# Loading 320 tokens of the first batch ahead, the first pair through hardware queues, norm steps moved forward, and the last store in halves: attention and SwiGLU feed-forward in one kernel

## The chip, the cores and the metric

The kernel runs on one core of one Trainium2 chip. The metric is device time in microseconds (us) of one execution. Every version was run several times, alternating with the kernel before on the same chip. The granted clock is the share of full speed that the chip let TensorE run at, as the trace records it. Each run has a state, fast or slow, judged by its time and granted clock. All times below are of fast runs. One run of the kernel before, first listed beside the first four experiments, took 452.8 us at a granted clock of 0.849. It was in the slow state and is left out.

A trace counts from the start of its span, which leaves out about 1.8 us of the timed execution (span 405.8 us in a run of 407.61 us). Times within a trace are compared with times within a trace, and run times with run times.

## The reference, cut to what matters

Eight batches of blockwise causal attention (8 heads, 576 tokens, head size 64, blocks of 64) feed an RMS norm and a SwiGLU feed-forward layer (512 to 1536 to 512).

```python
scores = scale * np.matmul(q, k.transpose(0, 1, 3, 2))      # (8, 8, 576, 576)
mask = block_i >= block_j                                   # blocks of 64
attn = softmax(where(mask, scores, -1e9))
x = (attn @ v).transpose(0, 2, 1, 3).reshape(4608, 512)
xn = x / sqrt(mean(x * x) + 1e-6) * rms_g
g = xn @ w_gate
out = (g * sigmoid(g) * (xn @ w_val)) @ w_out
```

## The kernel before

TensorE (PE) does everything large. Attention is done per pair of heads: transpose q and k, multiply scores, and let ScalarE (ACT) take the exponential into `PT`; the product with v follows. A norm chain then runs over the tokens: sums, squares, a turn on VectorE (DVE), a root by Newton steps, a spread into `st`, and a scaling that multiplies by a broadcast of `st` and writes `XT`. A `group()` is one feed-forward step of 16 matmuls, or one down projection. The hand-written order puts groups between the attention steps so that PE has work while ACT and DVE finish theirs. `later(n, ...)` puts a step n groups further on. The results of matmuls go to tiles in PSUM (`fps`, `sps`). Batch 0 has nothing before it, so its order holds zero matmuls, `fill(n)`, instead of groups.

```python
    WARM = 11
    ...
    def fill(n):
        f = ps_f.tile([P, 512], FP32, name="fps")
        for _ in range(n):
            nc.tensor.matmul(f, zero[:, 0:P], zero, start=True, stop=True)

    fill(WARM)
    load_pair(0, 0)                  # q and k of heads 0, 1: GpSimd DMAs that cast to bf16
    make_identity(nc, ident)
    for t in range(1, HP):
        load_pair(0, t)
    ...
    transpose_pair(0, 0, on_act="k")
    ...
    fill(2)
    scores(0, 0, "a")
    scores(0, 0, "b")
    transpose_pair(0, 1, on_act="k")
    scores(0, 0, "c")
    fill(1)
    ...                              # pairs 1 to 3, first values, norm of the first 256 tokens
    group()
    scores(1, 0, 2)
    transpose_pair(1, 1, on_act="qk")
    for u in range(HP):
        norm_scale("b", 0, 256, 320, u)     # "the second scaling": tokens 256 to 575
    mark(S)
    scores(1, 1, 0)
    group()
```

The last down projection ends with one copy of 128 x 512 and two stores, both issued by SyncE (SP).

## Time and profile before

| | before |
|---|---|
| runs beside the changed kernel | 408.19 us median (407.38 to 408.34, 4 runs) |
| span of the trace | 405.8 us |
| PE busy | 388.2 us (96%) |
| granted clock of the profiled run | 0.999 |

The lines that the prediction rests on stand in it, below. Two more lines mattered in the end. The first is the page's row of the granted TensorE clock, in tenths of full speed, for 40 equal slices. The second comes from ACT's timeline; its columns are start, length, engine, line, what was done, and in brackets how long the engine idled before and what released it.

```profile
PEclk9999999999999999999999999999999999999999
```

```profile
1.19 1.28 ACT L204 ACT_TABLE_LOAD   x1 [1.19 <-PEq L721]
```

The clock stays at full rate throughout. ACT's function table is loaded in the first 2.5 us, when nobody needs ACT. The trace puts it down to line 204, the copy after the first transposes, but it ran four us before that copy.

### The profile page before, as it was taken

What the parts mean: (1) busy time and instruction counts of PE and PEld (TensorE: products, weight loads), DVE (VectorE), ACT (ScalarE), POOL (GpSimd) and SP (SyncE); (2) the same over time, 40 slices, a digit from 0 to 9 for tenths busy, and PEclk for the clock granted to TensorE, in tenths of its full rate; (3) what the DMA queues carried; (4) which work ended last, traced back from release to release, by engine and by line L of the source; (5) the groups of instructions that cost most, each with busy time, mean ns of one, the idle gap of its engine ahead of it and who ended that gap; (6) DMA issues with size and microseconds to landing.
All of it is one profiled execution on the core that took longest, in us unless ns stands there. A gap on an engine that the chain in (4) does not pass through costs nothing.

```text
span 405.8 us, 7824 instructions
## 1 busy us (share of the span) xinstructions
PE 388.2 (96%) x3090; PEld 183.1 (45%) x3090; DVE 252.1 (62%) x619; ACT 197.9 (49%) x284; POOL 128.7 (32%) x181
## 2 busy tenths in 40 slices
PE   7889999998999999999999999999999999999995
PEld 3567665433444444344444444444434434444442
DVE  4788585677767654477627765667457768554430
ACT  4826771475457653465446654565455213332321
POOL 8828675645047063660068004200110010100000
PEclk9999999999999999999999999999999999999999
DMA  8999999999929498998089905500120010010112
GB/s 110 172 204 185 193 145 140 184 151 160 108 58 129 60 91 132 133 144 104 2 119 139 135 12 86 71 0 2 40 67 2 0 37 17 20 33 27 52 53 78
DMA packets 139764, 36.43 MB, mean 90 GB/s; under 512 B 129232, under 2 KB 136912, under 8 KB 139728
## 3 DMA queue, kind: packets, MB, share of 16 engines
q0 software_dynamic: 108448, 26.75, 66.9%
q1 hardware_dynamic: 30752, 9.18, 16.1%
q8 instruction: 24, 0.39, 0.4%
q14 instruction: 12, 0.10, 0.1%
q10 hardware_dynamic: 528, 0.00, 0.1%
HBM read 38.80 MB, written 9.44 MB: 119 GB/s over the span
## 4 chain that ended last, share of the span: by engine, by line
PE 81%; DVE 10%; ACT 3%; DMA 2%; POOL 1%; issue 1%; DVEq 0%; ACTq 0%; POOLq 0%
PE fps L457 41%; PE fps L473 22%; PE sps L241 6%; PE sps L290 4%; PE fps L330 3%; DVE HT L465 3%; DVE gs L463 3%; DVE XT L426 2%; ACT th L461 2%; DMA VB<-in_v_dram 2%; PE fps L290 2%; PE fps L433 1%; PE fps L381 1%; POOL nt L109 1%; ACT PT L250 1%
## 5 line engine op out<-in xcount | busy, mean ns | idle before, releaser
L457 PE MATMUL fps<-XT,WG 128*128 128x512 bf16 (+1 forms) x480 | 113.3, 359 | 2.9 <-DVE XT L426 2.5
L463 DVE SCALAR_TENSOR_TENSOR gs<-th,fps 128x512 bf16<-128x512 f32 x108 | 74.1, 686 | 61.7 <-ACT th L461 61.4
L250 ACT ACTIVATE PT<-sps 128x1024 bf16<-128x1024 f32 (+1 forms) x96 | 93.4, 988 | 38.9 <-PE sps L241 38.4
L457 PE MATMUL fps<-XT,WV 128*128 128x512 bf16 (+1 forms) x480 | 111.0, 358 | 0.0
L461 ACT ACTIVATE th<-fps 128x512 f32<-128x512 f32 x108 | 64.6, 598 | 73.5 <-PE fps L457 71.3
L473 PE MATMUL fps<-WO,HT 128*128 128x512 bf16 x432 | 97.6, 380 | 0.3 <-DVE HT L465 0.3
L465 DVE TENSOR_TENSOR HT<-gs,fps 128x512 bf16<-128x512 bf16 x108 | 74.3, 688 | 11.6 <-DVE gs L463 0.5
L457 PEld LDWEIGHTS <-WV 128*128 128x128 bf16 x480 | 46.9, 98 | 49.0 <-issue 3.2
L457 PEld LDWEIGHTS <-WG 128*128 128x128 bf16 x480 | 42.4, 98 | 50.0 <-issue 14.1
L473 PEld LDWEIGHTS <-HT 128*128 128x128 bf16 x432 | 41.3, 98 | 51.9 <-issue 3.2
L476 ACT ACTIVATE osb<-fps 128x512 f32<-128x512 f32 x36 | 21.5, 597 | 81.2 <-PE fps L473 78.3
L484 POOL DMA_DIRECT2D out_dram<-osb x22 | 12.7, 575 | 149.2 <-ACT osb L476 147.0
L123 POOL DMA_DIRECT2D VB<-in_v_dram x48 | 39.6, 848 | 17.3 <-PE sps L290 14.2
L426 DVE SCALAR_TENSOR_TENSOR XT<-OT,gscale,fps 128x64 bf16<-128x64 bf16 (+5 forms) x72 | 30.2, 477 | 21.2 <-PE fps L433 21.2
L241 PE MATMUL sps<-QT,KT 64*128 64x192 bf16 (+5 forms) x280 | 32.1, 308 | 1.9 <-ACT KT L204 0.9
L116 POOL DMA_DIRECT2D nt<-in_q_dram x30 | 26.2, 875 | 7.0 <-DMA VB<-in_v_dram 4.6
L116 POOL DMA_DIRECT2D nt<-in_k_dram x30 | 26.3, 876 | 5.8 <-DMA nt<-in_q_dram 1.6
L290 PEld LDWEIGHTS <-VB 128*64 128x64 bf16 x344 | 14.3, 109 | 14.6 <-issue 4.7
L223 DVE MEMSET PT<- 64x64 uint32 x95 | 9.1, 112 | 18.6 <-ACT PT L250 15.3
L316 DVE TENSOR_TENSOR SQ<-OT 128x512 bf16<-128x512 bf16 (+1 forms) x44 | 16.0, 374 | 6.4 <-ACT OT L314 5.5
L487 POOL DMA_DIRECT2D out_dram<-osb x12 | 6.6, 554 | 41.8 <-ACT osb L476 41.8
L241 PEld LDWEIGHTS <-KT 64*128 64x128 bf16 x280 | 8.7, 94 | 22.3 <-issue 17.1
(70 smaller groups left out, 221.6 us busy)
## 6 DMA issues: line engine op xcount, KB each, us to landing
out_dram<-osb POOLq DMA_DIRECT2D x22, 256.0 KB, 2.4
VB<-in_v_dram POOLq DMA_DIRECT2D x32, 128.0 KB, 5.6
nt<-in_q_dram POOLq DMA_DIRECT2D x24, 128.0 KB, 5.6
nt<-in_k_dram POOLq DMA_DIRECT2D x24, 128.0 KB, 6.0
WG<-in_moe_w_gate_dram POOLq DMA_DIRECT2D x4, 384.0 KB, 9.4
WV<-in_moe_w_val_dram POOLq DMA_DIRECT2D x4, 384.0 KB, 10.6
WO<-in_moe_w_out_dram POOLq DMA_DIRECT2D x4, 384.0 KB, 7.7
out_dram<-osb POOLq DMA_DIRECT2D x12, 128.0 KB, 2.6
```

The costliest lines, as they stand in the source:

```text
L116: nc.gpsimd.dma_start(out=nt[0:rows, 0:512].rearrange("p (h d) -> p h d", h=H), in_=src[b, :, c * P:c * P + rows, :].rearrange("h p d -> p ...
L123: nc.gpsimd.dma_start(out=vb[r:r + n, cc, :].rearrange("p (h d) -> p h d", h=H), in_=v[b, :, tok:tok + n, :].rearrange("h p d -> p h d"))
L241: nc.tensor.matmul(sp[:, a, o:o + w], KT[b][r, t, c * P:(c + 1) * P], QT[b][r, t, q0:q0 + w], start=True, stop=True, skip_group_check=True)
L250: nc.scalar.activation(out=pt[:, :, lo:lo + width], in_=sp[:, :, 0:width], func=AF.Exp, scale=SCALE)
L290: nc.tensor.matmul(ov[a * D:(a + 1) * D, o:o + w], vb[:, c, h * D:(h + 1) * D], rhs, start=(i == 0), stop=(i == len(chunks) - 1), skip_gro ...
L426: nc.vector.scalar_tensor_tensor(out=XT[:, u, y0:y0 + hi - lo], in0=OT[b][:, u, j + lo:j + hi], scalar=gscale[:, u:u + 1], in1=src[:, lo:h ...
L457: nc.tensor.matmul(acc[:, i * w:(i + 1) * w], wt[c][:, p, r * P:(r + 1) * P], XT[:, p, x0:x0 + w], start=(p == 0), stop=(p == HP - 1), ski ...
L461: nc.scalar.activation(out=th, in_=g, func=AF.Tanh, scale=0.5)
L463: nc.vector.scalar_tensor_tensor(out=gs, in0=th, scalar=1.0, in1=g, op0=ALU.add, op1=ALU.mult)
L465: nc.vector.tensor_mul(out=HT[n][:, m:m + k, lo:lo + w], in0=gs.rearrange("p (k w) -> p k w", k=k), in1=u.rearrange("p (k w) -> p k w", k=k))
L473: nc.tensor.matmul(po, HT[n][:, m, i * P:(i + 1) * P], WO[:, m, :], start=(m == 0), stop=(m == NMC - 1))
L476: nc.scalar.mul(out=osb, in_=po, mul=0.5)
```

## The change

The intent: start batch 0 earlier by handling only its first 320 tokens at first. The first pair of q and k comes as plain float32 through the hardware queues of SP and ACT and is cast on DVE and ACT. The last 256 tokens are loaded, transposed and scored later, between groups. The order of the second scaling, of batch 1's steps and of the norm chains ("tails") of batches 1 and 2 is tightened. The last store goes out in two column halves on two queues. The diff, cut to its core:

```diff
-    WARM = 11
+    CUT = 5 * BLK
+    WARM = 8
...
+    def load_plain(kind, hi):
+        eng, cast = (nc.sync, nc.vector.tensor_copy) if kind == "q" else (nc.scalar, nc.scalar.copy)
+        raw = obuf.tile([P, 512], FP32, name="osb")
+        for a in range(2):
+            eng.dma_start(out=raw[a * D:(a + 1) * D, 0:hi], in_=...)
+        return lambda: cast(out=nat_pairs(kind, 0)[:, 0, 0:hi], in_=raw[:, 0:hi])
...
-    load_pair(0, 0)
+    casts = [load_plain("q", CUT), load_plain("k", CUT)]
+    load_stretch("q", 0, 1, 0, CUT)
     make_identity(nc, ident)
-    for t in range(1, HP):
-        load_pair(0, t)
-    for c in range(5):
+    load_stretch("k", 0, 1, 0, CUT)
+    for c in range(3):
         load_v(0, c)
+    for kind in "qk":
+        load_stretch(kind, 0, 0, CUT, S)
...
+    A, Z = (0, CUT), (CUT, S)
+    for cast in casts:
+        cast()
+    transpose_pair(0, 0, "k", *A)
...
     scores(1, 0, 0)
     scores(1, 0, 1)
-    group()
-    scores(1, 0, 2)
-    transpose_pair(1, 1, on_act="qk")
     for u in range(HP):
         norm_scale("b", 0, 256, 320, u)
     mark(S)
+    group()
+    scores(1, 0, 2)
+    transpose_pair(1, 1, on_act="qk")
     scores(1, 1, 0)
     group()
     transpose_pair(1, 2, on_act="qk")
     scores(1, 1, 1)
-    group()
...
-    later(1, tail, 1, 4)
+    tail(1, 0, 1, 1, 1, 1, (2, 2, 3, 3, 3))
...
+        last = (n, i) == downs[-1]
+        step = DM // 2 if last else DM
+        for o in range(0, DM, step):
+            ...                     # matmuls, copy and stores of one half
+                    e = nc.scalar if last and j else eng
```

Of the eleven zero matmuls after the warm-up the changed kernel keeps ten, in other places: between the transposes of pair 1 and the root it has one, where the kernel before has six. Not shown are the rest of the new order of batch 0, a tail of batch 3 that also comes about a group earlier, one group each that is taken out of the order of batches 2 and 3 (its work comes later), and some constants and buffers that are made in another way.

> **What bounds the kernel now.** I read the page's busy table and slices first, then the busy time in stretches, then the PE timeline of the first 50 us, and last VectorE, the DMA issues and the end.
>
> ```profile
> PE 388.2 (96%) x3090; PEld 183.1 (45%) x3090; DVE 252.1 (62%) x619; ACT 197.9 (49%) x284; POOL 128.7 (32%) x181
> ...
> PE   7889999998999999999999999999999999999995
> ...
> 1.20:24.90 23.70, 20.19 (x318) 10.62 (x319) 15.36 (x66) 14.32 (x16) 18.96 (x33) 1.00 1.36 160
> 24.90:44.00 19.10, 17.76 (x278) 13.84 (x279) 16.14 (x44) 9.56 (x14) 13.06 (x19) 1.00 1.52 193
> ```
>
> TensorE is busy 388.2 of 405.8 us, so the end is TensorE's own work plus its waits and its filler. The work itself does not change (same scores, values, transposes and feed-forward groups), so I count only waste: waits and the zero matmuls of the helper `fill`. In the stretch to 24.90 us PE looks 85% busy (20.19 of 23.70), but much of that is filler. The PE timeline shows the stations of batch 0:
>
> ```profile
> 1.20 4.56 PE L145 MATMUL fps<-zero 128*128 128x512 bf16 x11 [1.20 <-DVE zero L139]
> ...
> 7.72 1.08 PE L199 MATMUL fps<-ident,nt 64*64 64x64 bf16 x36
> ...
> 13.76 0.30 PE L290 MATMUL fps<-PT,VB 128*64 128x256 bf16 x2
> ...
> 18.36 0.38 PE L352 MATMUL fps<-SQ,SEL 128*32 128x256 bf16 x4
> ...
> 20.07 0.58 PE L381 MATMUL fps<-w,GSUM 128*128 128x8 f32 x4 [0.47 <-DVE w L373]
> ...
> 24.91 1.10 PE L457 MATMUL fps<-XT,WG 128*128 128x256 bf16 x8 [0.18 <-DVE XT L426]
> ```
>
> Warm-up ends at 5.7, the second pair is transposed from 7.72, the first values start at 13.76, the squares' sums at 18.36, the root at 20.07, and the first feed-forward group runs from about 24.5 (its first rows) to 26.80. Real PE work done before 24.5, from the start-to-start steps of this timeline: transposes 4 x 0.68, twelve score steps of about 0.3, ends 0.25, first values 4 x 0.34, sums 0.56, squares 0.3, root 0.5, two later values 0.57 each, scaling 0.44: 10.9 us. So 13.6 us of the first 24.5 are waste. After 46 us the waits listed for PE total some 5 us, most of them 0.2 to 0.5 each.
>
> **What the Trainium skill says.** "DMA: Bandwidth & Descriptors", section "SWDGE vs HWDGE vs iDMA", says that a casting DMA has to go by GpSimd, a plain one may go by SP or ACT with faster setup: hence the plain first pair with an on-chip cast. The trace agrees as far as it goes: the only early hardware load, the small gscale, lands 2.1 us after issue, the first GpSimd loads 3.3 us, the next 4.5 and 4.7 us. The same page, "Issuing engines are not separate DMA queues", warns that the plain loads share the same engines; no run here shows yet how much they delay the rest. "TensorE: Matmul & The Clock Gate", Part 1, gives half clock for the first 3.4 us or so of activity; the trace agrees (warm-up weight loads 0.43 us apart to 5.0 us, 512-column matmuls 0.22 us apart later). Its "Architectural detail" calls VectorE and ScalarE strictly first in, first out, on which my largest term rests.
>
> **The change, part by part.**
>
> *First pair plain.* Two DMAs on each of SP and ACT should land at about 3.5 us (issue 0.7, a second issue 0.4 later, 2.1 to 2.4 to landing); casts (0.4) end by 4.4; the warm-up of 8 ends at 1.2 + 8 x 0.427 = 4.6. Pair 0's transposes start about 1.0 us earlier than 5.7. But pair 1 needs the stretch loads:
>
> ```profile
> nt<-in_q_dram POOLq DMA_DIRECT2D x1, 144.0 KB, 4.5
> nt<-in_k_dram POOLq DMA_DIRECT2D x1, 144.0 KB, 4.7
> ```
>
> These are the third and fourth GpSimd loads, issued at 3.02 and 3.56: landed at 7.5 and 8.26. In the changed kernel the third and fourth are the two halves of k's stretch, issued at the same times behind the identity; each moves 123 KB instead of 147. I expect 8.0 to 8.2. So the second pair starts where it does now, and only its copies are shorter (320 instead of 576 columns, 0.45 instead of 0.64 to 0.76).
>
> *Chain from there.* Per pair: transposes 0.39, copies 0.45 each, scores 0.33. Pair 1 scores 8.9, pair 2 10.5, pair 3 12.1, first values 12.4 (now 13.76), squares done 16.8 (now 18.75), root 18.1 (now 20.07). Two microseconds won, because only 320 tokens are handled.
>
> *Then ACT.* Between root and scaling ACT now carries eight copies of the last 256 tokens (about 0.28 each) and three exps (0.92 each). The second half of the copies waits behind two exps, and the scaling's PSUM buffers wait for those copies. Scaling starts at 22.3, the first group at 23.3 and ends at 25.75, with its last slice of XT late by 0.5. That is 1.05 us ahead of 26.80, but 2.3 us less work is done by then (two values, one more score step and others now follow, between the groups). There, the first group's corner memsets stand behind gs and HT on VectorE and cost a further 0.7. I reach "six groups done, batch 1's pair 0 scored" at 42.2; the present kernel has the same work behind it at 41.9 (group six ends 43.8, less 1.9 of work done earlier). Start: +0.3.
>
> *The second scaling.* It now comes right after group six, not one group and one transpose later. VectorE's order there:
>
> ```profile
> 36.17 0.69 DVE L463 SCALAR_TENSOR_TENSOR gs<-th,fps 128x512 bf16<-128x512 f32 x1 [0.27 <-ACT th L461]
> 36.97 0.69 DVE L465 TENSOR_TENSOR HT<-gs,fps 128x512 bf16<-128x512 bf16 x1
> 37.57 0.16 DVE L395 SCALAR_TENSOR_TENSOR z<-y 128x10 f32<-128x10 f32 x1
> ...
> 38.40 0.51 DVE L411 STREAM_TRANSPOSE st<-S 128x320 bf16<-128x320 bf16 x1
> ...
> 40.80 1.92 DVE L426 SCALAR_TENSOR_TENSOR XT<-OT,gscale,fps 128x320 bf16<-128x320 bf16 x4
> ```
>
> The group before began on PE at 34.48, and its st was done at 38.91, 4.43 us later. PE has 1.83 (group) and 0.52 (two scores) to fill that: a wait of 2.1. Then four scalings of 0.48 plus 0.3 of latency precede group seven's last slice, against 0.9 of PE work: 1.4 more. 3.5 in place of the present 0.8 (waits of 0.49 and 0.33): +2.7.
>
> *Batch 1's ends.* With one group fewer left, two transposes and two scores follow each other with no group between, and ACT has four copies and an exp (3.0 us) before the ends' product may start, PE 2.2 us: 1.3 instead of 0.45, +0.85.
>
> *Tighter tails of batches 1 and 2.* All steps lie one or two groups after the sums. Root to st took 3.1 us in batch 1 (70.35 to 73.46), one down projection hides 2.6: 0.45, plus 0.35 for the last XT slice and 0.2 for squares, less the 0.39 wait that goes; batch 2 similar. Together +1.0. Batches 4 and on keep their order.
>
> *The end.* Two 256-column halves cost PE 0.1 more; the last copy is 0.4 instead of 0.6, and the two last stores issue on two queues instead of one after the other:
>
> ```profile
> 401.33 0.60 ACT L476 ACTIVATE osb<-fps 128x512 f32<-128x512 f32 x1 [1.99 <-PE fps L473]
> 401.96 1.11 SPq L487 DMA_DIRECT2D out_dram<-osb  x2
> ```
>
> That saves half of 1.11 and a little transfer: -0.7 in all.
>
> Sum: 0.3 + 2.7 + 0.85 + 1.0 - 0.7 = +4.1, giving 412.4. I take off 1.4, because waits added by hand overlap (a PE that is late finds the next tile ready) and because tuned offsets suggest that somebody saw fewer stalls than I count: 411.0.
>
> **Rivals.** (1) The early start pays. If k's stretch lands at 6.5 because fewer bytes precede it, the whole chain moves 1 to 1.5 us left until the third chunk of v (about 11 us) holds it; with the waits half as long as I count, about 404 to 406. For it: the transfer rate sagged between 4.8 and 6 us in this trace without a visible reason, so there is room. Against: issue times on GpSimd are the same. (2) The clock falls back. The warm-up is shorter and PE idles until 8 us, so transposes and scores could run at half clock a second time; each link of the chain doubles its small PE part, 1 to 2 us more: 412 to 415. For it: little PE work before 8 us. Against: gaps are under 2 us, and gaps of 0.7 left the clock up. (3) The start is hidden anyway and only the end counts: 407.5. Against: the second scaling's order on VectorE is fixed and longer than PE's cover.
>
> **Range and chances.** All waste that PE has after 1.2 us is about 20 us, half of it in chains this change leaves, so a gain over 8 us is nearly excluded; a loss over 8 needs my stalls in full and a cold clock. The three rivals span 404 to 415, and I let the range hold both ends: 404.5 to 415. Faster 0.03, within 2% 0.92, slower 0.05.
>
> **What would show it.** Right: pair 1's k transposes wait for nt until about 8; squares near 16.5; first group near 23.3; PE idle about 2 us before the second scaling, released by st, and a second gap before group seven released by XT; the ends' product waiting for a KT copy for over 1 us; the last landing 0.7 us sooner after the last matmul. Wrong: k landing before 7, no wait at the second scaling, or the first group ending before 24.5.

## The result, and the profile after

| | median | fast runs | ratio to before | 95% interval |
|---|---|---|---|---|
| before | 408.19 us | 407.38 to 408.34 | | |
| after | 423.57 us | 423.18 to 424.23 | 1.0383 | 1.0362 to 1.0403 |

The change made the kernel slower by 15.4 us, far outside the predicted range. A ratio here is the mean time of one kernel's fast runs over the mean of the other's fast runs of the same rounds, so it is not quite the ratio of the medians.

Page of the kernel after: the busy line, and the granted clock in 40 slices of 10.55 us.

```profile
PE 395.2 (94%) x3060; PEld 189.1 (45%) x3098; DVE 249.9 (59%) x616; ACT 203.0 (48%) x301; POOL 128.1 (30%) x176
...
PEclk9579888999999999999999999999999999999999
```

PE is busy 7.0 us longer than before (395.2 against 388.2), although its real work is the same and it has four filler matmuls fewer. The second row says why: in the first 75 us the clock was granted only in part. The record steps between 1.00 and 0.50. I cut the trace at its steps, and one window ahead of each fall.

```profile
5.19:8.60 3.41, 1.77 (x30) 0.90 (x30) 2.41 (x12) 2.29 (x4) 3.41 (x6) 1.00 1.50 131
8.60:25.67 17.07, 13.39 (x214) 8.66 (x213) 8.47 (x34) 8.98 (x17) 11.39 (x17) 0.50 1.50 185
...
46.14:49.56 3.42, 1.35 (x12) 0.66 (x10) 2.54 (x8) 2.05 (x3) 1.64 (x2) 1.00 1.37 190
49.56:56.38 6.82, 6.19 (x59) 3.40 (x56) 3.36 (x7) 1.97 (x3) 4.47 (x7) 0.50 2.38 158
...
59.80:63.21 3.41, 2.25 (x77) 1.60 (x72) 0.95 (x4) 3.37 (x6) 0.00 (x0) 1.00 1.86 153
63.21:66.62 3.41, 3.41 (x18) 2.10 (x19) 0.69 (x1) 1.72 (x3) 0.00 (x0) 0.50 1.79 117
```

The columns are the window and its length, then the busy time (and instructions) of PE, PEld, DVE, ACT and POOL, then the clock, the DMA share and GB/s. Three times the clock falls to half, at 8.60, 49.56 and 63.21 us, for 17.07, 6.82 and 3.41 us. These lengths are 5, 2 and 1 times 3.41 us, and every edge lies on one grid of 3.41 us (from 25.67 to 49.56 it is 7 times 3.41). Just before each fall PE was busy 1.77, 1.35 and 2.25 us of 3.41 or 3.42: 52%, 40% and 66%. In the same first stretch (5.19 to 8.60) the kernel before was busy 3.08 us.

The PE timeline of the kernel after answers the stations shown in the prediction:

```profile
5.59 0.34 PE L232 MATMUL fps<-ident,nt 64*64 64x64 bf16 x10 [0.81 <-DVE nt L142]
7.18 0.34 PE L232 MATMUL fps<-ident,nt 64*64 64x64 bf16 x10 [1.24 <-ACT nt L142]
...
9.15 0.74 PE L232 MATMUL fps<-ident,nt 64*64 64x64 bf16 x20
...
19.61 0.53 PE L390 MATMUL fps<-SQ,SEL 128*32 128x256 bf16 x4
...
21.47 0.99 PE L419 MATMUL fps<-w,GSUM 128*128 128x8 f32 x4 [0.35 <-ACT QT L237]
...
49.18 0.89 PE L471 MATMUL fps<-st,SELB 128*128 128x320 bf16 x4 [2.07 <-DVE st L449]
50.11 2.60 PE L495 MATMUL fps<-XT,WG 128*128 128x256 bf16 x8
52.51 1.91 PE L495 MATMUL fps<-XT,WV 128*128 128x256 bf16 x8
...
57.16 0.39 PE L275 MATMUL sps<-QT,KT 64*128 64x512 bf16 x2 [1.10 <-ACT KT L237]
```

The first pair is not early: q's transposes start at 5.59 us and k's wait until 7.18, where the kernel before had both from 5.69 on. From 8.60 on the same instructions take longer than in the prediction's fence: the four squares' sums 0.53 instead of 0.38 us, the root's four matmuls 0.99 instead of 0.58. The first group starts at 27.58. At 49.18 the predicted wait for `st` is there, 2.07 us long. The clock fell at 49.56, and the second half of the group behind it, which waits for nothing, took 1.91 us, where the same eight matmuls at full clock take 1.04.

Why k came so late shows in ACT's timeline of the kernel after:

```profile
0.75 1.47 ACTq L138 DMA_DIRECT2D osb<-in_k_dram  x2
...
5.37 1.28 ACT L142 ACT_TABLE_LOAD   x1 [5.37 <-DMA osb<-in_k_dram]
6.67 0.46 ACT L142 CAST nt<-osb 128x320 bf16<-128x320 f32 x1
```

The table load now waits for the data of k and stands between its landing and its cast. The trace puts the load down to the line of the cast, as it was put down to the copy of line 204 before, but here it ran only when the cast's data had come. The Trainium skill's "ScalarE: Activation LUTs", "What ACT_TABLE_LOAD costs", gives about 1283 ns for a load; the trace agrees, 1.28 us in both kernels.

The end, on the timeline of the kernel after; the two rows are the issue of stores on two queues:

```profile
417.45 1.73 SPq L528 DMA_DIRECT2D out_dram<-osb  x2
...
418.72 0.50 ACTq L528 DMA_DIRECT2D out_dram<-osb  x1
```

The last matmul ends at 418.26 and the span at 422.07, 3.80 us later; before it was 401.25 and 405.85, 4.60 us. The end gained 0.8 us.

### The profile page after: what moved, and what is told of

Read it like the earlier page. It is cut to its first block, busy times and chain, and to the rows that moved or that the text cites. A ratio compares the mean times of both kernels' runs of the same rounds, so it can differ in the third digit from the quotient of the medians.

```text
span 422.1 us, 7790 instructions
## 1 busy us (share of the span) xinstructions
PE 395.2 (94%) x3060; PEld 189.1 (45%) x3098; DVE 249.9 (59%) x616; ACT 203.0 (48%) x301; POOL 128.1 (30%) x176
## 4 chain that ended last, share of the span: by engine, by line
PE 79%; DVE 13%; ACT 4%; issue 2%; DMA 1%; ACTq 0%; DVEq 0%
PE fps L495 40%; PE fps L520 20%; PE sps L275 6%; PE sps L324 4%; DVE XT L464 3%; DVE HT L503 3%; DVE gs L501 2%; PE fps L368 2%; PE fps L324 2%; ACT th L499 2%; PE fps L471 1%; PE fps L419 1%; DMA osb<-in_k_dram 1%; DVE OT L349 1%; PE fps L232 1%
## 5 line engine op out<-in xcount | busy, mean ns | idle before, releaser
L495 PE MATMUL fps<-XT,WV 128*128 128x512 bf16 (+1 forms) x477 | 112.4, 362 | 0.2
L520 PE MATMUL fps<-WO,HT 128*128 128x512 bf16 (+1 forms) x430 | 96.9, 373 | 1.3 <-DVE HT L503 0.3
L495 PEld LDWEIGHTS <-WV 128*128 128x128 bf16 x480 | 47.8, 99 | 49.9 <-issue 3.4
L524 POOL DMA_DIRECT2D out_dram<-osb x22 | 12.6, 575 | 187.0 <-ACT osb L522 187.0
L520 PEld LDWEIGHTS <-HT 128*128 128x128 bf16 x444 | 42.4, 98 | 50.7 <-issue 3.2
L522 ACT ACTIVATE osb<-fps 128x512 f32<-128x512 f32 (+1 forms) x37 | 21.7, 585 | 82.6 <-PE fps L520 76.0
L275 PE MATMUL sps<-QT,KT 64*128 64x192 bf16 (+5 forms) x280 | 33.9, 321 | 3.3 <-DVE KT L239 1.4
L354 DVE TENSOR_TENSOR SQ<-OT 128x512 bf16<-128x512 bf16 (+1 forms) x42 | 15.4, 379 | 8.1 <-ACT OT L347 7.3
L324 PE MATMUL sps<-PT,VB 128*64 128x512 bf16 (+3 forms) x160 | 15.9, 320 | 0.0
```

Of the source, the lines that this page charges most:

```text
L275: nc.tensor.matmul(sp[:, a, o:o + w], KT[b][r, t, c * P:(c + 1) * P], QT[b][r, t, q0:q0 + w], start=True, stop=True, skip_group_check=True)
L324: nc.tensor.matmul(ov[a * D:(a + 1) * D, o:o + w], vb[:, c, h * D:(h + 1) * D], rhs, start=(i == 0), stop=(i == len(chunks) - 1), skip_gro ...
L495: nc.tensor.matmul(acc[:, i * w:(i + 1) * w], wt[c][:, p, r * P:(r + 1) * P], XT[:, p, x0:x0 + w], start=(p == 0), stop=(p == HP - 1), ski ...
L520: nc.tensor.matmul(po[:, 0:step], HT[n][:, m, i * P:(i + 1) * P], WO[:, m, o:o + step], start=(m == 0), stop=(m == NMC - 1))
L522: nc.scalar.mul(out=osb[:, o:o + step], in_=po[:, 0:step], mul=0.5)
```

## The experiments

**Theory:** a large part of the loss comes from TensorE falling to half clock, because the new order leaves PE idle where the old one kept it busy with real or zero matmuls. Late casts, a blocked table load and new waits make the rest. **Rivals:** the shorter warm-up alone loses the clock; or the clock is a side effect and the waits cost the time whatever the clock does.

### Longer warm-up

```diff
-    WARM = 8
+    WARM = 18
```

> The changed kernel with 18 warm-up matmuls instead of 8, nothing else: PE is kept busy through the two early waits (4.8 to 5.6 and 5.9 to 7.2 us). Theory 'clock' (the early idle time makes the granted clock fall to half at 8.6 us, and most of the loss follows from that): no half-clock stretch between 8.6 and 25.7 us, first feed-forward group at 25 to 26 instead of 27.6, time 419 to 421 (some 3 us less than 423.6). Rival 'waits' (the time goes to waits in the new order, the low clock only fills gaps that would be there anyway): under 1 us less, 423. The second fall of the clock, after the wait at 47 to 49 us, stays in both.

Measured: 421.50 us (421.17 to 422.53), ratio 1.0332 (1.0315 to 1.0350), clock 0.976 to 0.983. The clock's first fall moved from 8.6 to 16.2 us, and the second stayed, at about 50. Two us came back. A longer warm-up only delays the first fall: the 3.41 us before it hold waits of 0.83 us before the scores of pair 3 and 1.35 us before the first values of pair 2, and PE was busy 1.23 us in them.

### Nine zero matmuls where the second scaling waits

They write into the PSUM tile that the scaling's first matmul overwrites.

```diff
         bc = ps_f.tile([P, 512], FP32, name="fps")
+        if key == "b" and t == 0:
+            for _ in range(9):
+                nc.tensor.matmul(bc, zero[:, 0:P], zero, start=True, stop=True)
```

> The changed kernel with nine zero matmuls put into the PSUM tile of the second scaling just before it, where PE waits 2.07 us for st; the wait itself stays, PE is only kept busy in it. Theory 'clock': the fall of the granted clock at 49.6 us goes (and the one at 63.2 perhaps with it), group seven takes 3 us instead of 4.2; 420 to 421, 2.5 to 4 us less. Rival 'waits': nothing gained, 423 to 424, since the matmuls shorten no wait.

Measured: 421.06 us (420.88 to 421.35), ratio 1.0318 (1.0302 to 1.0334), clock 0.978 to 0.987. The falls at 49 and 63 us are gone, and the run is 2.5 us shorter, although PE still can't go on before the same `st`. So the wait had cost its own length and half clock behind it. The first half-rate stretch was another too: the view shows 1.00 up to 16.1 us, yet ten transposes at 5.6 us took 0.48 us instead of 0.34. The trace's clock record begins only at 12.68 us in this run (at 5.19 in the kernel after), and the view prints 1.00 for what comes before it. But the start did not help this run: its first group began at 27.98 us, 0.4 later than in the kernel after. From there to the end it took 391.3 us, against 394.5. So the two later falls had cost about 3.2 us.

### Both

> Both at once: 18 warm-up matmuls and nine zero matmuls before the second scaling. Theory 'clock': mean granted clock 0.99 or more and 415 to 418; what then remains over 408.2 is the new waits (second scaling about 2.7, ends about 0.9, tails about 1, less 0.7 at the end: 412) and the late plain loads. Rival 'waits': 422 to 423.

Measured: 420.85 us (418.28 to 421.41), ratio 1.030 (1.0262 to 1.0338), clock 0.984 to 0.995. The two gains do not add. In the profiled run the clock fell at about 14 us, ahead of the first values, and came back between 27 and 28. The fastest run, 418.28, has the highest clock, 0.995.

### Shorter warm-up in the kernel before

```diff
-    WARM = 11
+    WARM = 8
```

> The kernel before with 8 warm-up matmuls instead of 11, nothing else: PE then idles from 4.8 to about 5.6 us, but nothing else is late. Theory 'clock' in its simple form (the shorter warm-up alone loses the clock): a half-clock stretch appears early and the time rises by 1 to 4 us. Rival (it takes the second wait too, for the table load behind the k load): the clock stays up, 408 to 408.5.

Measured: 407.75 us (407.55 to 408.58), ratio 0.9998 (0.9980 to 1.0016), clock 0.997 to 1.0. The short warm-up alone loses nothing, so that rival is out.

### All fillers

Zero matmuls stand wherever the changed kernel leaves PE idle: a warm-up of 16, three before the scores of pairs 2 and 3, five and two before the first values of pairs 2 and 3, nine before the second scaling.

```diff
-    WARM = 8
+    WARM = 16
...
+        for _ in range(3 if (b, step) == (0, "a") and t > 1 else 0):
+            nc.tensor.matmul(sp[:, 0, :], zero[:, 0:P], zero, start=True, stop=True, ...)
...
+        for _ in range({2: 5, 3: 2}.get(t, 0) if width == 256 and j0 == 0 else 0):
+            nc.tensor.matmul(ov, zero[:, 0:P], zero, start=True, stop=True, ...)
...                                 # and the nine of above
```

> The changed kernel with zero matmuls in every early wait: 16 warm-ups, three before each of the scores of pairs 2 and 3, five and two before the first values of pairs 2 and 3, nine before the second scaling. They go into the PSUM tile that the waiting matmul will overwrite, so no buffer is added and no wait shortened. Theory 'clock': with PE kept busy the granted clock stays up after the warm-up; the stations come to squares 18.5, first group 26, second scaling 47, time 416 to 418, and what is left above 408.2 is order and late loads. Rival 'waits': 420 to 421 as in the run with both fillers, although the clock stays up, because the filler takes the place of idle time and ACT and DVE set the pace.

Measured: 417.61 us (417.32 to 417.88), ratio 1.0230 (1.0212 to 1.0249), clock 0.998 to 1.0. With the clock at full rate 6.0 us come back, out of 15.4. In its trace the first group starts at 25.12 us, 2.5 earlier than in the kernel after; with the 3.2 us of the later falls that makes 5.7 of the 6.0. The clock theory holds, and so does a limit to it: 9.4 us are not the clock.

### All fillers, and the table loaded early

```diff
     casts = [load_plain("q", CUT), load_plain("k", CUT)]
+    tiny = small.tile([P, 1], BF16, name="tiny")
+    nc.scalar.copy(out=tiny, in_=zero[:, 0:1])
...
-    WARM = 16
+    WARM = 11
```

> The same with 11 warm-ups and a one-column ACT copy of the zero tile just after k's two plain loads are issued, so that the table load (1.28 us) is done while the loads are in flight, and not after they have landed (5.37). Expected: k's cast starts at 5.4 instead of 6.67, pair 0's second transposes at 5.9 instead of 7.2. If these were what holds pair 1, all stations move 1 us earlier than in the run with all fillers and the time falls by 1 us. Rival: pair 1's k lands at about 8 whatever pair 0 does, so at most 0.5 us is gained.

Measured: 416.45 us (416.15 to 417.20), ratio 1.0207 (1.0191 to 1.0223), clock 0.998 to 1.0. The early table is worth 1.2 us, about the 1.28 us of its load. The shorter warm-up is a second change, but with 16 it was k's cast, and not the warm-up, that the transposes of pair 0's k waited for (0.69 us). This version runs the changed order without either accident, so its trace shows what the order itself costs. From its PE timeline:

```profile
12.26 0.64 PE L332 MATMUL fps<-PT,VB 128*64 128x256 bf16 x12
...
23.36 1.31 PE L506 MATMUL fps<-XT,WG 128*128 128x256 bf16 x8
...
42.49 2.12 PE L480 MATMUL fps<-zero 128*128 128x512 bf16 x9
44.62 0.70 PE L482 MATMUL fps<-st,SELB 128*128 128x320 bf16 x4
...
51.03 0.39 PE L280 MATMUL sps<-QT,KT 64*128 64x512 bf16 x2 [1.51 <-ACT KT L239]
...
55.76 0.29 PE L303 MATMUL sps<-QT,KT 64*64 64x64 bf16 x12 [0.37 <-ACT PT L289]
56.84 0.22 PE L303 MATMUL sps<-QT,KT 64*64 64x64 bf16 x4 [0.79 <-ACT KT L239]
```

The stations of batch 0 are those of the prediction: first values 12.26 (predicted 12.4), first group 23.36 (23.3), and the root, not shown, at 18.21 (18.1). The scaling, at 21.95 (22.3), is the one that is off by more than 0.15 us. The nine zeros stand for the wait at the second scaling, and four waits of 0.19 to 0.23 us for `XT`, not shown, follow. Then come a wait of 1.51 us for a copy of KT and 0.37 and 0.79 us before the ends' product.

### The second scaling moved back

It goes behind the third score step and the next transposes, as in the kernel before; the nine zeros go.

```diff
     scores(1, 0, 1)
+    scores(1, 0, 2)
+    transpose_pair(1, 1, on_act="qk")
     for u in range(HP):
         norm_scale("b", 0, 256, 320, u)
     mark(S)
-    group()
-    scores(1, 0, 2)
-    transpose_pair(1, 1, on_act="qk")
     scores(1, 1, 0)
     group()
+    group()
     transpose_pair(1, 2, on_act="qk")
```

> As the last, but the second scaling is moved behind the scores and the transposes of batch 1's pair 1, as the kernel before has them (one PE score step of 0.3 and 0.7 of transposes to cover the wait), and the nine zero matmuls before it go. Theory 'order': the wait of 2.1 us falls to about 1.1, and ACT gets its copies earlier, so the wait for KT after it (1.1 to 1.5 us in the changed kernel) goes as well: 2 us less than the last. Rival: the wait only moves to XT, under 1 us less.

Measured: 414.67 us (413.62 to 415.84), ratio 1.0162 (1.0129 to 1.0194). The median is 1.8 us lower. The four runs fall into two: 413.6 and 413.7 at a clock of 0.999 and 1.0, 415.7 and 415.8 at 0.995 and 0.990. So 2.8 us lower at full clock. The profiled run was one of the disturbed ones, with half clock from about 20 to 23 and 47 to 50.5 us. Its PE timeline has the wait in two other places:

```profile
44.77 0.40 PE L280 MATMUL sps<-QT,KT 64*128 64x320 bf16 x4 [0.93 <-ACT PT L289]
...
47.03 0.69 PE L479 MATMUL fps<-st,SELB 128*128 128x320 bf16 x2 [0.68 <-ACT QT L239]
```

PE now waits for ACT, which has the exponentials and the copies of the transposes in this stretch. The wait of 1.51 us for KT is gone, as expected, and part of the wait for `st` was exchanged and not removed.

### Tails of batches 1 and 2 as before

On top of the last version:

```diff
-    tail(1, 0, 1, 1, 1, 1, (2, 2, 3, 3, 3))
+    later(1, tail, 1, 1, 2, 3, 3, 4, (4, 4, 5, 5, 6))
...
-            tail(2, 0, 1, 1, 1, 2, (3, 3, 4, 4, 4))
+            later(1, tail, 2, 1, 2, 3, 3, 4, (4, 4, 5, 5, 6))
```

> The last version (fillers, early table load, second scaling behind pair 1) with the tails of batches 1 and 2 put back to the offsets of the kernel before (one group later, scalings four to six groups after the sums). Theory 'tails': the waits for st, for XT and for the squares between 60 and 125 us go, 1 to 1.6 us less than 414.7. Rival: the feed-forward groups are one ahead, so they run out of scaled tokens and a down projection or nothing takes the place; same or slower.

Measured: 417.75 us (415.54 to 418.23), ratio 1.0219 (1.0189 to 1.0249), clock 0.983 to 0.992. It was slower, not faster. The waits for `XT` and for the squares between 60 and 131 us are gone, as the theory said (1.0 us in the version that it is built on). But two things mix: all its runs have a lower clock than the version that it is built on at its best, and undoing the tails alone made a new wait of 3.3 us for `st` at 123 us, which the traces of before and after don't have. Batch 3's tail and the group dropped in batches 2 and 3 were not put back; whether the new wait comes from that was not tested. The test doesn't support the theory that the tighter tails cost time by themselves, and it doesn't size them.

### First pair by GpSimd, all fillers

The plain path is taken out of the "all fillers" version; pair 0 comes in the stretch loads with the other pairs.

```diff
-    casts = [load_plain("q", CUT), load_plain("k", CUT)]
-    load_stretch("q", 0, 1, 0, CUT)
+    casts = []
+    load_stretch("q", 0, 0, 0, CUT)
     make_identity(nc, ident)
-    load_stretch("k", 0, 1, 0, CUT)
+    load_stretch("k", 0, 0, 0, CUT)
```

> The version with all fillers (16 warm-ups, 417.6), but pair 0 loaded by GpSimd in the same stretch DMAs as the others, cast in flight; no plain loads, no casts on VectorE and ACT, and the table load is early again because nothing makes it wait. Theory 'plain path pays': pair 0's k now lands with the stretch at about 8 and the chain starts 0.5 to 1 us later than with the early table load (416.5): 417 to 418. Rival 'plain path costs as much as it brings' : equal to 416.5 within 0.5, since pair 1 waits for the same stretch.

Measured: 420.07 us (418.97 to 421.45), ratio 1.0288 (1.0258 to 1.0318), clock 0.996 to 1.0. PE timeline:

```profile
7.82 0.21 PE L232 MATMUL fps<-ident,nt 64*64 64x64 bf16 x1 [1.08 <-DMA nt<-in_k_dram]
8.61 0.34 PE L232 MATMUL fps<-ident,nt 64*64 64x64 bf16 x9 [0.58 <-DMA nt<-in_k_dram]
```

k of pair 0 lands at about 8.6 us and everything follows it. Within this order the plain path is worth 2.5 us by the medians (420.07 less 417.61), even with the table load in its way. But these runs fall into two as well: 419.0 and 419.1 at a clock of 0.999 and 1.0, 421.1 and 421.5 at 0.996. At full clock it is worth 1.4 us. The likely reason for its worth is that the stretch loads bring all four pairs together, so that without the plain path no pair is early; only the late k is shown.

### The kernel before without its later zero matmuls

All six later calls of `fill`, eleven matmuls, are taken out; the warm-up stays.

```diff
-    fill(2)
     scores(0, 0, "a")
...
-    fill(3)
     for u in range(HP):
         norm_scale("a", 0, 0, 256, u)
```

> The kernel before without the eleven zero matmuls that it issues between the steps of batch 0 (the 11 warm-ups stay): nothing else differs, so order, loads and waits are those of the kernel before. Theory 'clock': PE's early idle time alone loses the granted clock: a half-clock stretch of one or more pieces of 3.4 us between 8 and 30 us, and 1 to 4 us more than 408.2. Rival: they only fill idle time; the clock stays and the time falls by up to 1 us, as their own PE time goes.

Measured: 409.82 us (408.63 to 410.12), ratio 1.0026 (0.9998 to 1.0053), clock 0.987 to 0.991. The busy time in stretches of this kernel, with the columns of above:

```profile
15.20:19.00 3.80, 3.54 (x54) 2.11 (x58) 2.58 (x10) 2.24 (x3) 3.80 (x6) 0.55 1.26 175
25.10:29.30 4.20, 3.67 (x17) 2.30 (x17) 3.35 (x11) 0.60 (x1) 1.31 (x3) 0.59 1.31 202
```

The clock fell twice, and each half-rate stretch was busy. This shows, in the kernel before and without any other part of the change, that the clock falls when these matmuls go. What it costs is less sure: removing instructions that compute nothing cost 1.7 us by the medians, but the interval just includes no change. One of the eleven runs of the kernel before beside it had a clock of 0.990, and it took 410.29 us.

### Only the last store in halves

The part of the diff in `ffn_down`, alone, on the kernel before.

> The kernel before with only the last store in column halves on two queues. Expected from the working: 0.7 us less, 407.5, a ratio of 0.998. Rival: the last landing is set by the slower of two concurrent stores, and nothing is gained.

Measured over five rounds: 407.29 us (406.88 to 408.38), ratio 0.9982 (0.9967 to 0.9997). From the timeline of its end:

```profile
401.12 1.73 SPq L490 DMA_DIRECT2D out_dram<-osb  x2
...
402.38 0.50 ACTq L490 DMA_DIRECT2D out_dram<-osb  x1
```

The last matmul ends at 401.93 and the span at 405.67: 3.74 us against 4.60, so 0.9 us less, much as in the changed kernel. By the medians the gain is 0.9 us.

### The halves, and the whole first pair plain, in the old order

q and k of pair 0, all 576 tokens, plain in one DMA each, table loaded early, WARM 13; pair 1 moves to the front of GpSimd's loads. The order of the work is that of before.

```diff
-    load_pair(0, 0)
+    for kind, src, eng in (("q", q, nc.sync), ("k", k, nc.scalar)):
+        RAW[kind] = const.tile([P, S], FP32, name="RAW" + kind)
+        eng.dma_start(out=RAW[kind], in_=...)
+    nc.scalar.copy(out=tiny, in_=zero[:, 0:1])
+    load_pair(0, 1)
     make_identity(nc, ident)
-    for t in range(1, HP):
+    for t in range(2, HP):
...
+    nc.vector.tensor_copy(out=NAT["q", 0, 0], in_=RAW["q"])
+    nc.scalar.copy(out=NAT["k", 0, 0], in_=RAW["k"])
     transpose_pair(0, 0, on_act="k")
```

> The kernel before with the last store in halves, and pair 0 (all 576 tokens) loaded plain through the two hardware queues, cast on VectorE and ACT, table load early, 13 warm-ups; GpSimd starts with pair 1. If what the plain path is worth is that GpSimd's first two loads are pair 1's, they land at about 5.5 to 6.5 instead of 7.5 and 8.3, pair 1's transposes start about 1 us earlier than 7.7, and the time is 406.3 to 406.8. Rival: pair 0 lands later than 5.3 (147 KB more on the same engines), its cast and transposes move to 6.5 and nothing is gained: 407.3 as with the halves alone.

Measured over five rounds: 407.14 us (406.83 to 408.00), ratio 0.9975 (0.9955 to 0.9994). That is 0.15 us from the halves alone, within their scatter. The second pair's transposes in its PE timeline:

```profile
7.91 0.76 PE L207 MATMUL fps<-ident,nt 64*64 64x64 bf16 x36
```

They start at 7.91 us instead of 7.72, and the first pair's at 5.87 instead of 5.69. The plain loads of 288 KB each landed 3.5 and 3.8 us after issue, and the cast comes on top; the first GpSimd loads of before land 3.3 us after issue and need none. The first half of the expectation did come true: pair 1's q and k landed at 5.95 and 6.84 us instead of 7.54 and 8.28. It gained nothing, because the second pair's transposes follow pair 0's scores in PE's order, and those started at 7.36 instead of 7.18. This version and the halves alone are the only two that beat both kernels, by about 1 us or 0.2%.

## Why the prediction was wrong

The prediction gave +2.7 us (4.1 less 1.4); the runs gave +15.4. Two ways to take that apart agree.

By run medians, step by step from after: half clock 6.0 (423.57 to 417.61), table load 1.2 (to 416.45), and 8.3 for the order of the work, net of the gain at the end (416.45 less 408.19). The prediction's terms for that order came to 4.15, so of the 12.7 us by which it missed, 6.0 are the clock, 1.2 the table load, 4.1 terms of the order that were missing or too small, and 1.4 a deduction. By the trace of the version with all fillers and the early table, whose span of 414.3 us is 8.5 above before:

| stretch | before, us | after | fillers and table | cost in the latter | predicted |
|---|---|---|---|---|---|
| second pair's transposes start | 7.72 | 9.15 | 7.58 | | 8.0 to 8.2 |
| first values start | 13.76 | 14.95 | 12.26 | | 12.4 |
| first group starts | 24.91 | 27.58 | 23.36 | | 23.3 |
| six groups done, batch 1's pair 0 scored | 41.9 (equal work) | 47.1 | 42.5 | +0.6 | +0.3 |
| from there to the first down projection | 22.9 | 32.5 | 29.4 | +6.5 | +3.55 |
| from there to the last matmul's end | 336.45 | 338.6 | 338.6 | +2.2 | +1.0 |
| from there to the end | 4.60 | 3.80 | 3.80 | -0.8 | -0.7 |

The last-but-one column sums to 8.5; the prediction's to 4.15, before it took 1.4 off.

**The step that failed most: "The clock falls back", as a rival sized at 1 to 2 us and dismissed with "gaps are under 2 us, and gaps of 0.7 left the clock up".** It happened three times in the profiled run, for 27.3 us in all (17.07, 6.82 and 3.41), and cost 6.0 us. The argument failed because it looked at single gaps. Up to the first fall no gap after the warm-up was longer than 1.24 us, but the 3.41 us before it held that one and half of another (0.81), and left PE busy 52%. Nor were all gaps under 2 us: the wait of 2.1 us that the prediction itself forecast at the second scaling came, and the second fall with it. The present kernel's eleven later zero matmuls, which I counted as waste, were what held the clock: without them the kernel before fell to half clock too. For the first fall the size was not far off (2.5 us by the first group); I missed that the later falls hit feed-forward groups, where PE is the bound (1.91 instead of 1.04 us for half a group at 52.51).

**"Two DMAs on each of SP and ACT should land at about 3.5 us; casts end by 4.4."** The first DMA of each queue did land when expected, 2.3 and 2.6 us after issue, but the second ones landed at 5.0 (q) and 5.3 (k), 3.6 and 3.9 us after theirs, and that issue came 0.6 and not 0.4 later. The estimate had used the small gscale load, alone on its queue, 2.1 us. The casts were of the expected size (0.46 us), but k's ended at 7.13 because of the table load, which the prediction doesn't mention. The load stood in the trace of before, where it lies ahead of all data; which instruction carries it was not asked.

**The second scaling, "+2.7".** The mechanism was right: PE waited 2.07 us for `st` (predicted 2.1). From 42.49 to 48.44 us in the fillers-and-table version, less the scaling's 0.55 and the group's 1.83, is 3.57 us of wait, and 3.5 were predicted for it. But I then took off the present kernel's 0.8. Those waits lie before 43.8 us, so they were in the 41.9 already: the term should have stood at +3.5. Moving the scaling back won 1.8 us by the medians and 2.8 at full clock, and ran into waits for ACT.

**Not foreseen:** the wait of 1.51 us for a KT copy after the second scaling's stretch (1.10 in the changed kernel, at half clock before it). ACT reaches that copy only after an exponential and QT's copy. The squares' sums of batch 1 took 0.89 instead of 0.42 us. With 3.57 for the scaling, 1.51, the ends' 0.7 and these 0.5, 6.3 of the 6.5 us are named.

**Batch 1's ends, "+0.85".** Right: waits of 0.37 and 0.79 against 0.45 before, +0.7.

**The tails, "+1.0".** Measured +2.2 from the first down projection to the last matmul. In the fillers-and-table version 1.4 of them are idle time of PE in that stretch (7.9 against 6.5 us) and 0.8 longer busy time. The two traces place the idle time: up to 131 us, the waits for `w`, `st`, `XT` and the squares' sums (those of 0.1 us and more) are 2.0 us there and 0.5 in before. So the forecast waits came, 1.5 us of them for 1.0. What another order of the tails would save stays open, as the experiment that undoes them made a new wait; the 0.8 is not explained.

**Batch 0's chain, "two microseconds won".** Right in the main, at full clock: first values, squares, root and first group are within 0.15 us, and the whole start was a small loss, as predicted (+0.6 for +0.3). One link was wrong: pair 1's transposes were to wait for k until about 8 us. In the fillers-and-table version k's stretch landed at 6.7 and 7.35 us, PE waited for no load there, and the first group still began at 23.36: the earlier landing of k was absorbed later in the chain. So part of the agreement is luck, and rival 1 is out. The prediction also put the present kernel's first group at 24.5, where its own line has 24.91, and the waits after 46 us at some 5 us, where the view of PE's waits from 46 us on comes to 6.8; no term rested on either.

**The end, "-0.7".** Right, here (-0.8) and alone.

**"I take off 1.4, because waits added by hand overlap."** Nothing in the trace had supported it. At full clock the forecast waits came at about their full length or more (3.57 us for 3.5, 0.7 for 0.85, 1.5 for 1.0), so there was nothing to take off.

**What stays open: the rule by which the clock falls.** The Trainium skill, "TensorE: Matmul & The Clock Gate", Part 1, describes a free-running window of 3413 ns and half clock "after ≥1 idle window". The trace agrees with the window: every edge lies on its grid. It does not agree that a window must be idle: windows at 52%, 40% and 66% busy were followed by falls. No sharp threshold fits either, because in the same trace one from 114.4 to 117.8 us, 67% busy, was not followed by a fall, and two windows at half clock of about 90% (3.06 and 3.05 us) had different outcomes, the first staying at half and the second rising. Cut on the grid of its own clock record, each of the 14 kept traces fits two bounds, though. All 14 falls came after a window in which PE was busy 2.62 us or less of 3.41, and every window at full clock with 1.86 us or less was followed by a fall; between 1.90 and 2.62 us both happened. The ends of matmuls are modelled in the trace, and their busy time may not be what the clock is granted on. The runs also differ among themselves. In thirteen of the traces the clock record begins between 3.9 and 6.9 us, in one at 12.68, so the same work is cut into windows at different places.

## What to carry to other kernels

Zero matmuls in a tuned order may be holding the clock, so take none out, and open no gap, without looking at PE's busy share over 3.4 us stretches rather than at single waits (here no stretch above 2.62 of 3.41 us was followed by a fall). A first load that is moved to another engine's queue must be followed to that engine's first instruction: a table load or another instruction put in front of it can inherit the wait. Add predicted waits up as they are, and put each reference moment on the same work before subtracting.

## What the Trainium skill lacked or had wrong

- "TensorE: Matmul & The Clock Gate", Part 1: the table gives half clock after an idle window. Here windows in which PE was busy 1.77, 1.35 and 2.25 of 3.41 us were followed by half clock. No section of the page says what share is enough. The table also gives full clock after one busy window. Here that held for all eleven windows at half clock with 3.24 us and more, but one at 3.06 of 3.41 us busy (18.84 to 22.25) left the clock at half.
- "ScalarE: Activation LUTs", "What ACT_TABLE_LOAD costs": the cost is right (1.28 us). The page doesn't say that the load can take up the wait of the instruction that it precedes: it ran at 1.19 us before and at 5.37 us after, behind the DMA of k.
- "DMA: Bandwidth & Descriptors", "SWDGE vs HWDGE vs iDMA": the page's faster setup of plain loads doesn't tell when they land under load. Of two plain loads of 80 KB on a queue the first landed 2.3 and 2.6 us after issue and the second 3.6 and 3.9, and loads of 288 KB each 3.5 and 3.8, with GpSimd's loads under way. The load of 2 KB for gscale took 2.1 us alone on its queue and 4.3 behind k's two.
- No page that I read says that a trace's clock record can begin late (at 5.19 us in the kernel after, at 12.68 in one run), so that a view shows 1.00 before it, although the warm-up's matmuls stand 0.43 us apart there and later ones 0.22.
